# Transposes of queries, pooled keys and values moved from TensorE to DMA in a fused attention and gated layer kernel

## The chip, the cores and the metric

The kernel runs on one core of a Trainium2 chip. The metric is the device time of one launch in microseconds; each run is one launch, and the number given for a kernel is the median of its runs.

## The reference

Two layers run one after the other, the second on the first one's result. All inputs and the output are float32.

```python
# q (4, 12288, 128); kv (4, 384, 32, 128); w_sr (128, 128)
kv_pool = kv.reshape(B, H // 4, 4, W // 4, 4, C).mean(axis=(2, 4))
k = v = kv_pool.reshape(B, -1, C) @ w_sr          # 768 keys a batch; values are the same numbers
a = softmax(q @ k.transpose(0, 2, 1) / sqrt(C))
x = (a @ v).reshape(49152, 128)
h = x @ w_in                                      # w_in (128, 2048)
out = (h * sigmoid(1.702 * h)) @ w_out            # w_out (2048, 128)
```

## The kernel before

**Groups and chunks.** The 49152 queries are 96 groups of 512 (24 a batch). In the attention layer a group meets 6 chunks of 128 keys, in the second layer 16 chunks of 128 hidden units. For each chunk TensorE does a "fill" into PSUM, a matmul of 512 columns (L350 in `fill_attn`, L596 in `fill_moe`). ScalarE takes two or three chunks at a time through exp (L352) or through the activation (L598) and writes bf16 into the large SBUF buffer `ag`, which holds 102 chunks. TensorE later "drains" them: for attention twelve matmuls of 129 columns for three key chunks (L363; the 129th column sums the weights), for the second layer one matmul of 512 columns for each chunk (L606). VectorE normalises the attention result into `x` (L386, L389), and transposes the final result from PSUM (L617); SP stores it (L619). Work goes in two rounds: attention of groups 0 to 47, their second layer, then the same for 48 to 95.

**Work that VectorE does in ScalarE's place.** The chunks of groups 48 to 51 (`early`), nine others (`rolling`) and 17 chunks of the second layer (`lent`) go through a polynomial on VectorE (L431 to L475).

**A planner written in Python** sets the order on every engine while the program is built. It keeps estimated clocks `now` (TensorE), `end[p]` (ScalarE's p-th activation) and `dve`, in units of one 512-column matmul, and places drains and other TensorE work between fills as long as the next fill still comes in time:

```python
FIXED, CHUNK, SWITCH, HANDOVER, EVACUATE = 0.295, 1.978, 6.0, 1.0, 4.5
...
limit = end[-1] - len(seq[n + 3][1]) - HANDOVER if n + 3 < len(seq) else 1e9
```

An activation of n chunks is taken to last `FIXED + CHUNK * n`. A fill may start half a `HANDOVER` after its two banks' last activation, and the activation half a `HANDOVER` after the fill. All engines take their instructions strictly in that order; a semaphore wait on one holds up what stands behind it.

**Queries.** TensorE needs them transposed, channel by token. `load_q` brings tiles of four groups in as bf16, and `transpose_q` turns one group with four TensorE transposes and a copy by VectorE (L236, L242); this serves tiles 0, 1 and 2, so groups 0 to 11. Tiles from 3 on go another way: `cast_q` (L209, issued by POOL) casts them from float32 into the DRAM buffer `q_bf`, and `load_qT` (L215, issued by SP) reads that back with a DMA transpose. `TURN` says at which group that is issued. The casts of tiles 3, 4 and 5 are in POOL's queue from the start.

**Keys and values.** `w_sr` is scaled by 1/16. In batches 0 and 1 `pool_chunk` (L139) pools a chunk by 16 narrow matmuls, and `key_and_value` (L161, L162) makes the key chunk and the value chunk from the result with one matmul each. In batches 2 and 3 DMAs with accumulation add up the rows in SBUF (`add_kv`, L173), VectorE adds the last two (`sum_kv`, L179), and for each half batch `transpose_pooled` (L184, four TensorE transposes), `make_k` (L192) and `make_v` (L199, three matmuls) follow with a copy by VectorE after each. These three are handed to the planner in `extras`, and it places them between fills. Values sit in `vs` with tokens on partitions, keys in `kTs` with channels on partitions.

**Other traffic on SP.** `x` is put away to DRAM (`put_away`, L503) and brought back transposed (`bring_back`, L509) in pieces of six groups, in the second layer of round one between groups 9 and 18.

Of the kernel before, what the change touches and what calls it, by code (L numbers as in the profile page):

```python
# [24 lines left out]
def kernel(  # L25
    ctx, tc, q, kv, w_sr, moe_w_in, moe_w_out, out,
):
    nc = tc.nc
# [20 lines left out]
    q_flat = q.rearrange("b n c -> (b n) c")  # L49
    x_bf = nc.dram_tensor("x_bf", (B * N, C), BF, kind="Internal").ap()  # L50
    q_bf = nc.dram_tensor("q_bf", (B * N, C), BF, kind="Internal").ap()

    kv_r = kv.rearrange("b (ch p) (a w) c -> b a ch p (w c)", p=128, a=2)

# [4 lines left out]
    R = 2  # L59
    XS = NS // R  # L60
    EARLY = 4
    AG = 102

    cpool = ctx.enter_context(tc.tile_pool(name="const", bufs=1))
# [33 lines left out]
    def acc_bf():  # L98
        return acc().bitcast(BF)
# [16 lines left out]
    HC = H // 128  # L116
    h = J // 2
    kv_tiles, kv_sums, pooled, pTs, kTs, vs = {}, {}, {}, {}, {}, {}

    def new_keys(b):  # L120
        kTs[b] = kvres.tile([128, J], BF, name="kT")

        vs[b] = kvres.tile([128, JC, C + 8], BF, name="v")
        nc.vector.memset(vs[b][:, :, C:C + 1], 1.0)

    def load_chunk(b, jc):

        a, ch = divmod(jc, HC)
        t = x_tile(XS - 1 - jc)
        nc.gpsimd.dma_start(out=t, in_=kv_r[b, a, ch])  # L130
        kv_tiles[b, jc] = t.rearrange("p (wp w1 c) -> p w1 wp c", w1=r, c=C)

    def pool_chunk(b, jc):

        ps = acc()
        t = kv_tiles.pop((b, jc))
        for wp in (0, 2, 1, 3) if (b, jc) == (0, 0) else range(4):
            for w in range(r):
                nc.tensor.matmul(ps[:, 32 * wp:32 * wp + 32], t[:, w, wp, :], sum4,  # L139
                                 start=(w == 0), stop=(w == r - 1))  # L140
        pTs[b, jc] = kvtmp.tile([128, 128], BF, name="pTc", bufs=2)
        nc.vector.tensor_copy(pTs[b, jc], ps[:, 0:128])

    def key_chunk(b, jc):
        if jc == 0:
# [22 lines left out]
    def add_kv(b, n):  # L168
        i, w = divmod(n, r)
        if n == 0:  # L170
            kv_sums[b] = kvsum.tile([Hp, 2, Wp, C], F32, name="kvs")
        for i2 in range(2):
            nc.gpsimd.dma_start(out=kv_sums[b][:, i2], in_=kv_p[b, i, w, :, i2],  # L173
                                **({"accum_op": ADD} if n else {}))
# [3 lines left out]
        pooled[b, a] = kvtmp.tile([Hp, 4, C], BF, name="pooled")  # L178
        nc.vector.tensor_tensor(pooled[b, a], t[:, 0], t[:, 1], ADD)  # L179

    def transpose_pooled(b, a):
        ps = acc_bf()[:, 0:h].rearrange("p (a b) -> p a b", a=4)
        for wp in range(4):
            nc.tensor.transpose(ps[:, wp, :], pooled[b, a][:, wp, :], ident[:Hp, :Hp])  # L184
        pTs[b, a] = kvtmp.tile([128, h], BF, name="pT")
        nc.vector.tensor_copy(pTs[b, a], ps.rearrange("p a b -> p (a b)"))

    def make_k(b, a):
        ps = acc()
        if a == 0:  # L190
            new_keys(b)
        nc.tensor.matmul(ps[:, :h], w_sr_sb, pTs[b, a], start=True, stop=True)  # L192
        nc.vector.tensor_copy(kTs[b][:, a * h:(a + 1) * h], ps[:, :h])

    def make_v(b, a):
        ps = acc()
        pT = pTs.pop((b, a))
        for k in range(K):
            nc.tensor.matmul(ps[:, k * C:(k + 1) * C], pT[:, k * 128:(k + 1) * 128], w_sr_sb,  # L199
                             start=True, stop=True)  # L200
        nc.vector.tensor_copy(vs[b][:, a * K:(a + 1) * K, 0:C], ps[:, :h].rearrange("p (k c) -> p k c", k=K))
        for jc in range(a * K, a * K + K):
            vs[b, jc] = True

# [10 lines left out]
        nc.sync.dma_start_transpose(out=qTs[s], in_=q_bf[s * SG:(s + 1) * SG, :])  # L215


    QS = 3
    qs = [x_tile(XS - 1 - JC - s) for s in range(QS)]

    def load_q(s, lo, hi):
# [31 lines left out]
    for jc in range(2, JC):  # L253
        load_chunk(0, jc)
    load_q(1, 2, 4)
    for s in range(2, QS):
        load_q(s, 0, 2)
        load_q(s, 2, 4)
    cast_q(3)
    cast_q(4)  # L260

# [32 lines left out]
            nc.tensor.matmul(banks[:32, 2, :], ones, ones.unsqueeze(1).broadcast_to([128, 16, 32]),  # L294
                             start=True, stop=True)

    w_in_sb = cpool.tile([128, d_ff], BF)
    w_out_sb = cpool.tile([128, FCH, C], BF)

    ag = agpool.tile([128, AG, 512], BF, name="ag")  # L300
    warm(13)
# [44 lines left out]

    def fill_attn(chunks, ps):
        for k, (i, jc) in enumerate(chunks):
            rhs = qTs[i // 4][:, 0, (i % 4) * G:(i % 4 + 1) * G]
            nc.tensor.matmul(ps[:, k, :], kTs[i // GB][:, jc * 128:(jc + 1) * 128], rhs,  # L350
                             start=True, stop=True)
        nc.scalar.activation(place([("a",) + c for c in chunks]), ps, AF.Exp, scale=scale)  # L352

    def drain_attn(t, a):

        nonlocal kept
        i, u, k = t // 4, t // TS, t % TS
        split = u < SPLIT
        if k == 0 and (a == 0 or split):
            av_of[u] = acc(("av", u))  # L360
# [58 lines left out]
    def early_step():  # L419
        nonlocal steps  # L420
        on_dve(next(steps))
        if steps.gi_frame.f_locals["last"]:
            steps = None
            made[early_todo.pop(0)] = dve

    def early_exp(ps, out):
        last = False
# [49 lines left out]
        yield 3.5  # L477

    raw = None
    made, used = {}, []  # L480
    steps, early_todo = None, [c for c in rolling if c[0] < early[0]]
    early_todo += [(i, jc) for i in early for jc in range(JC)]
# [37 lines left out]
        nc.vector.memset(one, 0.0)  # L520
        nc.gpsimd.memset(one, 0.0)  # L521

    TURN = {6: 3, 7: 4, 8: 5, 20: 6, 21: 7, 22: 8, 25: 9, 32: 10, 35: 11, 40: 12}
    CAST = {0: [5], 13: [6], 14: [7], 15: [8], 16: [9], 26: [10, 11], 27: [12]}
    CAST_MOE = {20: 13, 21: 14, 22: 15, 23: 16, 33: 17, 34: 18, 35: 19, 36: 20, 37: 21, 38: 22, 39: 23}

    def background(i):

        first_round = i < GB * 2
        s = TURN.get(i, NS) if first_round else i // 4 + 3 if i % 4 == 0 else NS  # L530
        if s < NS:
            load_qT(s)
        if i in CAST:
            gate()
            for s in CAST[i]:
                cast_q(s)
        if i in (10, 12):
            gate()
            for jc in range(i % 10 * 3 // 2, i % 10 * 3 // 2 + 3):
                load_chunk(1, jc)  # L540
        if 0 <= i - 16 < JC:
            extras.append((key_and_value, 1, i - 16))
        if 0 <= i - 15 < JC:
            extras.append((pool_chunk, 1, i - 15))
        if i in (28, 33, 38):
            put_away(0, (i - 28) // 5)
        if i in (31, 36, 41):
            bring_back(0, (i - 31) // 5)
        if i == 28:
            gate()  # L550
            nc.gpsimd.dma_start(out=w_in_sb, in_=moe_w_in)
        if i == 29:
            gate()
            nc.gpsimd.dma_start(out=w_out_sb, in_=moe_w_out.rearrange("(o p) c -> p o c", p=128))

    def background_moe(g):
# [18 lines left out]
        for b, lo in ((2, 2), (3, 24)):  # L575
            if lo <= g < lo + 8:
                gate()
                add_kv(b, g - lo)
            if g in (lo + 10, lo + 12):
                use_kv(b, (g - lo - 10) // 2)  # L580

    def use_kv(b, a):
        nonlocal extra_at
        sum_kv(b, a)
        on_dve(3.5)
        extra_at = max(extra_at, dve + 1.5)
        extras.extend([(transpose_pooled, b, a), (make_k, b, a), (make_v, b, a)])

    extras = []

# [120 lines left out]
    def prepare(p):  # L711
# [3 lines left out]
        for i, jc in part:  # L715
            if (kind, i) not in begun:
                begun.add((kind, i))
                (background if kind == "a" else background_moe)(i)
            while kind == "a" and ((key_and_value, i // GB, jc) in extras or (transpose_q, i) in extras):
                f, *args = extras.pop(0)  # L720
                now = max(now, free[next_acc()]) + COST[f][0]
                f(*args)
                free[last_acc] = copied(f)
# [13 lines left out]
        13: [(key_and_value, 0, 4)],  # L737
        15: [(pool_chunk, 0, 5)],
        16: [(key_and_value, 0, 5), (later, 6)],
        17: [(later, 7)],  # L740
        18: [(later, g) for g in range(8, 12)]}

    FIXED, CHUNK, SWITCH, HANDOVER, EVACUATE = 0.295, 1.978, 6.0, 1.0, 4.5
    COST = {pool_chunk: (1.9, 2.6), key_chunk: (0.3, 2.4), value_chunk: (0.3, 2.4),
            transpose_q: (1.05, 4.2), early_fill: (1.0, 5.5), key_and_value: (0.55, 3.5),
            transpose_pooled: (0.9, 3.6), make_k: (0.8, 3.2), make_v: (0.8, 3.7)}
    COPY = {pool_chunk: 1.5, key_chunk: 1.5, value_chunk: 1.5, key_and_value: 2.8, transpose_q: 3.2}  # L750
    SMALL = 0.26
    RECIPROCAL = 8.2
    PAUSE = 4.0
# [15 lines left out]
    def fill(p):  # L769
# [13 lines left out]
        lo = K * (p % 2)  # L783
        (fill_attn if kind == "a" else fill_moe)(part, banks[:, lo:lo + len(part), :])
        if p >= 2:
            now = max(now, end[p - 2] + HANDOVER / 2)
        now += len(part)
        begin = max(now + HANDOVER / 2, end[p - 1] if p else 0.0)
        if p and kind != seq[p - 1][0]:
            begin += SWITCH  # L790
        end.append(begin + FIXED + CHUNK * len(part))
# [5 lines left out]
    for n in range(len(seq)):  # L797
        fill(n + 2)
        jobs(n + 3)
        while True:  # L800
            room = room_ahead()
            limit = end[-1] - len(seq[n + 3][1]) - HANDOVER if n + 3 < len(seq) else 1e9
            bank = free[next_acc()]
            f = None
            if extras and now >= max(extra_at, bank):
                f, *args = extras[0]
            if steps and dve <= now + 2.0:
                early_step()
            near = todo and todo[0][0] == "m" and todo[0][2] > 10
# [4 lines left out]
            if f:  # L814
                now = max(now, bank) + COST[f][0]
                f(*args)
                free[last_acc] = dve + 1.0 if f is early_fill else copied(f)
                if f in (transpose_pooled, make_k, make_v):
                    on_dve(2.5)
                extra_at = max(now + PAUSE, dve + 1.5 if f in (transpose_pooled, make_k, make_v) else 0.0)  # L820
                if f is early_fill:
                    pass
                else:
# [69 lines left out]
```

## Time and profile before

| what | value |
|---|---|
| median of 3 runs | 948.33 us (948.24 to 948.73) |
| span of the profiled execution, first to last instruction | 946.7 us |
| TensorE busy | 933.9 us |
| ScalarE busy | 933.5 us |
| VectorE busy | 575.1 us |
| granted TensorE clock | 1.000 |

The profiled execution has no separate time of its own; its span is 1.63 us below the median of the runs, which stands for what lies around the first and the last instruction. "PE" is TensorE, "PEld" its weight loads, "ACT" ScalarE, "DVE" VectorE, "POOL" GpSimd, "SP" the engine that issues most DMAs. Ends of matmuls are modelled, and matmuls overlap: one of 512 columns has a duration of 379 ns in the profile, and the next starts some 216 ns after it. Activations overlap too: a full-size one has a mean duration of about 1490 ns and the next starts about 1340 ns after it. So the busy shares of these two do not tell which of them waits. A row of a stretch of time reads: the stretch, its length, busy time and number of instructions of PE, PEld, DVE, ACT and POOL, granted clock, share of the DMA engines, GB/s. A DMA has a time from its issue to its landing, when its semaphore is complete.

### The profile page before, as it was taken

How to read it: one execution, taken by the hardware profiler on the slowest of the kernel's cores; microseconds unless marked ns; L12 is line 12 of the kernel's file. 1: busy time of each engine (PE TensorE's matmuls, PEld its weight loads, DVE VectorE, ACT ScalarE, POOL GpSimd, SP SyncE). 2: the span in 40 equal slices, each digit the busy share in tenths (PEclk: the TensorE clock that was granted, in tenths of full speed). 3: DMA queues.
4: the chain of work that ended last, by engine and by line, in shares of the span. 5: the costliest groups of instructions: out<-in, count | busy, mean ns of one | idle time of the engine just before them, and what ended most of it. 6: DMA issues, size and time to landing. Idle time of an engine off the chain costs nothing.

```text
span 946.7 us, 15374 instructions
## 1 busy us (share of the span) xinstructions
PE 933.9 (99%) x6200; PEld 502.5 (53%) x6314; DVE 575.1 (61%) x1091; ACT 933.5 (99%) x709; POOL 66.5 (7%) x115
## 2 busy tenths in 40 slices
PE   8999999999999999999999999999999999999998
PEld 4677776444444444444446777744444444444444
DVE  5753653011678776667765765376767766777651
ACT  6999999999999999999999999999999999999998
POOL 3101001330000232000000000000000000000000
PEclk9999999999999999999999999999999999999999
DMA  9997943999867799865335683552222222222222
GB/s 210 195 207 168 181 92 52 130 163 170 164 117 114 119 147 119 127 99 87 56 58 105 138 170 84 119 123 42 36 39 40 38 41 34 44 34 45 34 45 46
DMA packets 372856, 95.46 MB, mean 101 GB/s; under 512 B 346720, under 2 KB 370400, under 8 KB 372320
## 3 DMA queue, kind: packets, MB, share of 16 engines
q1 hardware_dynamic: 344000, 62.36, 36.9%
q0 software_dynamic: 28512, 31.99, 22.3%
q8 instruction: 49, 0.80, 0.3%
q14 instruction: 23, 0.19, 0.1%
q10 hardware_dynamic: 272, 0.13, 0.0%
HBM read 52.49 MB, written 48.76 MB: 107 GB/s over the span
## 4 chain that ended last, share of the span: by engine, by line
PE 97%; ACT 1%; DMA 1%; issue 1%; DVE 0%; POOL 0%; POOLq 0%
PE banks L606 35%; PE banks L596 34%; PE banks L363 14%; PE banks L350 12%; ACT ag L352 1%; PE banks L415 1%; DMA x<-in_kv_dram 1%; PE banks L139 0%; PE banks L409 0%; PE banks L634 0%; PE banks L236 0%; POOL x L222 0%; PE banks L161 0%; PE banks L294 0%; PE banks L192 0%
## 5 line engine op out<-in xcount | busy, mean ns | idle before, releaser
L598 ACT ACTIVATE ag<-banks 128x1536 bf16<-128x1536 f32 (+1 forms) x509 | 681.1, 1489 | 0.0
L596 PE MATMUL banks<-x,w_in_sb 128*128 128x512 bf16 x1476 | 405.8, 379 | 1.7
L606 PE MATMUL banks<-ag,w_out_sb 128*128 128x512 bf16 x1477 | 402.6, 379 | 1.7
L352 ACT ACTIVATE ag<-banks 128x1536 bf16<-128x1536 f32 (+2 forms) x192 | 245.6, 1421 | 3.5 <-PE banks L236 2.3
L606 PEld LDWEIGHTS <-w_out_sb 128*128 128x128 bf16 x1520 | 148.3, 98 | 177.2 <-issue 0.2
L596 PEld LDWEIGHTS <-w_in_sb 128*128 128x128 bf16 x1519 | 147.1, 98 | 171.3 <-issue 0.7
L617 DVE STREAM_TRANSPOSE o_sb<-banks 128x512 f32<-128x512 f32 x95 | 68.1, 717 | 171.4 <-PE banks L606 166.9
L363 PEld LDWEIGHTS <-ag 128*128 128x128 bf16 x2268 | 145.5, 98 | 44.6 <-issue 0.3
L363 PE MATMUL banks<-v,ag 128*128 128x129 bf16 x2268 | 163.0, 220 | 0.2
L350 PE MATMUL banks<-qT,kT 128*128 128x512 bf16 x498 | 145.0, 379 | 3.5 <-ACT ag L352 0.5
L442 DVE SCALAR_TENSOR_TENSOR ea<-ea,eb 128x512 f32<-128x512 f32 x132 | 90.4, 685 | 3.7 <-DVE ea L442 0.7
L386 DVE RECIPROCAL rec<-banks 128x3 f32<-128x3 f32 x124 | 22.3, 180 | 85.3 <-PE banks L363 84.9
L389 DVE TENSOR_TENSOR x<-banks,rec 128x384 bf16<-128x384 f32 x124 | 69.1, 557 | 4.3
L350 PEld LDWEIGHTS <-kT 128*128 128x128 bf16 x543 | 45.8, 98 | 25.9 <-issue 2.0
L473 DVE RECIPROCAL eb<-ea 128x256 f32<-128x256 f32 x34 | 57.6, 1724 | 0.5
L466 DVE SCALAR_TENSOR_TENSOR ea<-ea,eb 128x512 f32<-128x512 f32 x68 | 46.5, 683 | 1.9
L173 POOL DMA_DIRECT2D kvs<-in_kv_dram x32 | 40.4, 1323 | 19.3 <-DMA kvs<-in_kv_dram 17.1
L431 DVE TENSOR_SCALAR ea<-banks 128x512 f32<-128x512 f32 x33 | 22.8, 692 | 29.6 <-PE banks L415 29.2
L521 POOL MEMSET gate_tile<- 1x1 f32 x38 | 3.4, 89 | 325.8 <-DVE gate_tile L520 325.8
L453 DVE TENSOR_SCALAR qT<-banks 128x512 f32<-128x512 f32 x17 | 11.8, 692 | 20.7 <-PE banks L409 20.6
L437 DVE SCALAR_TENSOR_TENSOR eb<-eb,ea 128x512 f32<-128x512 f32 x33 | 22.8, 691 | 0.9
L444 DVE SCALAR_TENSOR_TENSOR ag<-ea,ee 128x512 bf16<-128x512 f32 x24 | 16.6, 691 | 1.2
(83 smaller groups left out, 286.3 us busy)
## 6 DMA issues: line engine op xcount, KB each, us to landing
out_dram<-o_sb SPq DMA_DIRECT2D x380, 64.0 KB, 2.0
kvs<-in_kv_dram POOLq DMA_DIRECT2D x32, 384.0 KB, 6.3
q_bf<-in_q_dram POOLq DMA_DIRECT2D x21, 512.0 KB, 6.6
x_bf<-x SPq DMA_DIRECT2D x13, 768.0 KB, 5.6
x<-in_kv_dram POOLq DMA_DIRECT2D x11, 512.0 KB, 10.4
x_bf<-x SPq DMA_DIRECT2D x6, 384.0 KB, 4.6
x<-in_q_dram POOLq DMA_DIRECT2D x5, 256.0 KB, 15.3
x<-in_kv_dram SPq DMA_DIRECT2D x1, 1024.0 KB, 5.0
```

Source lines behind the costliest of these rows:

```text
L173: nc.gpsimd.dma_start(out=kv_sums[b][:, i2], in_=kv_p[b, i, w, :, i2], **({"accum_op": ADD} if n else {}))
L350: nc.tensor.matmul(ps[:, k, :], kTs[i // GB][:, jc * 128:(jc + 1) * 128], rhs, start=True, stop=True)
L352: nc.scalar.activation(place([("a",) + c for c in chunks]), ps, AF.Exp, scale=scale)
L363: nc.tensor.matmul(av_of[u][:, k * (C + 1):(k + 1) * (C + 1)], weights(("a", i, jc))[:, o:o + T], vs[i // GB][:, jc, 0:C + 1], start=(jc = ...
L389: nc.vector.tensor_tensor(to, ps[:, :, 0:C], rec.unsqueeze(2).broadcast_to([128, TS, C]), MUL)
L442: nc.vector.scalar_tensor_tensor(a, a, COEFFS[k], b, ADD, MUL)
L466: nc.vector.scalar_tensor_tensor(a, a, COEFFS[k], b, ADD, MUL)
L473: nc.vector.reciprocal(b[:, m:m + 256], a[:, m:m + 256])
L596: nc.tensor.matmul(ps[:, k, :], w_in_sb[:, fc * 128:(fc + 1) * 128], x[:, g % (4 * XS) * G:(g % (4 * XS) + 1) * G], start=True, stop=True)
L598: nc.scalar.activation(place([("m",) + c for c in chunks]), ps, AF.Gelu_apprx_sigmoid)
L606: nc.tensor.matmul(o_of[g], w_out_sb[:, fc, :], weights(("m", g, fc)), start=(fc == 0), stop=(fc == FCH - 1))
L617: nc.vector.transpose(o_sb, o_of.pop(g))
```

## The change

Four things change. First, tile 2 of the queries (groups 8 to 11) is no longer loaded and turned on TensorE: it goes by `cast_q(2)`, in the place of its loads on POOL, and by `load_qT(2)` on SP, issued at group 5. Second, for batches 2 and 3 the pooled sums are written to a DRAM buffer (`put_pooled`) and read back with a DMA transpose (`turn_pooled`); `make_k` waits for it. The steps come at one group's distance: sum and write, transpose, `make_k`. Third, the values of batches 1, 2 and 3 are no longer made by a matmul: since they are the keys' own numbers, the finished keys are written to DRAM (`put_k`) and read back transposed, a chunk at a time (`turn_k`). All of these DMAs are issued by SP. Fourth, the planner's times: `FIXED` goes from 0.295 to 0.24; a fill may start `RELEASE` = 0.3 after the banks' last activation (was 0.5); an activation begins `LATENCY` = 0.95 after the fill (was 0.5); the margin in `limit` is 1.2 (was 1.0).

The diff also has a way to pool batch 1 by additions on VectorE (`add_chunk`, `pool_added`), which `ADDED = ()` leaves unused, and it joins the two weight tiles into one buffer. Batch 1 is still pooled by the narrow matmuls, a chunk a group, each followed by its key.

```diff
-    for s in range(2, QS):
-        load_q(s, 0, 2)
-        load_q(s, 2, 4)
+    cast_q(2)
     cast_q(3)
     cast_q(4)
...
-    TURN = {6: 3, 7: 4, 8: 5, 20: 6, 21: 7, 22: 8, 25: 9, 32: 10, 35: 11, 40: 12}
+    TURN = {5: 2, 6: 3, 7: 4, 8: 5, 20: 6, 21: 7, 22: 8, 25: 9, 32: 10, 35: 11, 40: 12}
...
-    def transpose_pooled(b, a):
...
+    def put_pooled(b, a):
+        nc.sync.dma_start(out=pool_bf[b, a].rearrange("w h c -> h w c"), in_=pooled[b, a])
+
+    def turn_pooled(b, a):
+        pTs[b, a] = kvtmp.tile([128, 1, h], BF, name="pT")
+        nc.sync.dma_start_transpose(out=pTs[b, a], in_=pool_bf[b, a].rearrange("w h c -> (w h) c"))
+
+    def put_k(b, a):
+        jc = slice(a * K, a * K + K)
+        nc.sync.dma_start(out=k_bf[b, jc].rearrange("j c t -> c j t"),
+                          in_=kTs[b][:, a * h:(a + 1) * h].rearrange("c (j t) -> c j t", t=128))
+
+    def turn_k(b, a):
+        for jc in range(a * K, a * K + K):
+            turned_v.add((b, jc))
+            nc.sync.dma_start_transpose(out=vs[b][:, jc:jc + 1, 0:C], in_=k_bf[b, jc])
...
+    def key_alone(b, jc):
...
+        nc.tensor.matmul(ps[:, 0:128], w_sr_sb, pTs.pop((b, jc)), start=True, stop=True)
...
-    def make_v(b, a):
...
-        if 0 <= i - 16 < JC:
-            extras.append((key_and_value, 1, i - 16))
-        if 0 <= i - 15 < JC:
-            extras.append((pool_chunk, 1, i - 15))
+        for a in range(2) if first_round else ():
+            if (1, a) in stored:
+                stored.remove((1, a))
+                turn_k(1, a)
+            if (1, a * K) not in turned_v and all((1, jc) in vs for jc in range(a * K, a * K + K)):
+                put_k(1, a)
+                stored.add((1, a))
...
-            if g in (lo + 10, lo + 12):
-                use_kv(b, (g - lo - 10) // 2)
+            a, step = divmod(g - lo - 9, 3)
+            if 0 <= a < 2 and step == 0:
+                sum_kv(b, a)
+                on_dve(3.5)
+                put_pooled(b, a)
+            if 0 <= a < 2 and step == 1:
+                turn_pooled(b, a)
+            if 0 <= a < 2 and step == 2:
+                extras.append((make_k, b, a))
+            if 1 <= a < 3 and step == 0:
+                put_k(b, a - 1)
+            if 1 <= a < 3 and step == 1:
+                turn_k(b, a - 1)
...
-        18: [(later, g) for g in range(8, 12)]}
...
-    FIXED, CHUNK, SWITCH, HANDOVER, EVACUATE = 0.295, 1.978, 6.0, 1.0, 4.5
+    FIXED, CHUNK, SWITCH, HANDOVER, EVACUATE = 0.24, 1.978, 6.0, 1.0, 4.5
+    RELEASE, LATENCY, MARGIN = 0.3, 0.95, 1.2
...
-            now = max(now, end[p - 2] + HANDOVER / 2)
+            now = max(now, end[p - 2] + RELEASE)
...
-        begin = max(now + HANDOVER / 2, end[p - 1] if p else 0.0)
+        begin = max(now + LATENCY, end[p - 1] if p else 0.0)
...
-            limit = end[-1] - len(seq[n + 3][1]) - HANDOVER if n + 3 < len(seq) else 1e9
+            limit = end[-1] - len(seq[n + 3][1]) - MARGIN if n + 3 < len(seq) else 1e9
```

## The prediction

> **What bounds the kernel now.** I read the page first, then stretches of a late stage, then single instructions. The page shows two engines that look full:
>
> ```profile
> span 946.7 us, 15374 instructions
> ...
> PE 933.9 (99%) x6200; PEld 502.5 (53%) x6314; DVE 575.1 (61%) x1091; ACT 933.5 (99%) x709; POOL 66.5 (7%) x115
> ...
> PE 97%; ACT 1%; DMA 1%; issue 1%; DVE 0%; POOL 0%; POOLq 0%
> ```
>
> The chain names TensorE, but its ends are modelled, so I count instead. In the table of stretches PEld's count is the number of matmuls:
>
> ```profile
> 700.00:800.00 100.00, 99.47 (x455) 45.33 (x464) 70.01 (x98) 100.00 (x75) 0.00 (x0) 1.00 0.26 40
> 800.00:900.00 100.00, 99.53 (x456) 45.32 (x463) 73.53 (x102) 100.00 (x76) 0.00 (x0) 1.00 0.25 38
> ```
>
> 464 matmuls of 512 columns in 100 us are one each 215.6 ns, which is also the distance between neighbours: no gap is left. The same sum over the run: 3632 matmuls of 512 columns x 215.6 ns, 2304 of 129 columns (L363) x 56.4 ns, and 18.4 us of small ones make 931.4 us. TensorE ends at 943.4 us, so it idles for 12.0 us: 9.8 before 75 us, 2.2 in all the rest. From 75 us on, a microsecond of TensorE work or waiting is a microsecond of the run.
>
> ScalarE is close behind. Full-size ACTIVATEs start at least 1.330 us apart (1.335 where nothing holds them up). The sum of what lies over 1.330 (0.904 and 0.477 for the smaller ones) is 18.4 us: 3.4 at the start, 4.2 at three table loads, and most of the rest where the activation starts 630 ns after the weight load of its last matmul, the least the trace has. There ScalarE waits for TensorE, though its groups show "idle 0.0".
>
> Before 35 us DMA and ScalarE also limit. The lines for what follows, each one instruction:
>
> ```profile
> L215 SPq DMA_TRANSPOSE qT<-q_bf x1: 4773/4773/4773, 29.2 to 29.2; - x1
> ...
> DMA to landing us min/median/max: 7.0/7.0/7.0
> ...
> L619 SPq DMA_DIRECT2D out_dram<-o_sb x1: 505/505/505, 298.5 to 298.5; - x1
> ...
> DMA to landing us min/median/max: 5.9/5.9/5.9
> ...
> L509 SPq DMA_TRANSPOSE x<-x_bf x1: 3390/3390/3390, 231.0 to 231.0; - x1
> ...
> DMA to landing us min/median/max: 6.3/6.3/6.3
> ```
>
> The first is today's earliest query transpose, the second a store issued just after a query cast, the third a transpose that the new one must queue behind.
>
> **What is removed.** TensorE loses 16 query transposes (16 x 56 ns = 0.90 us), 6 value matmuls of batch 1 (0.34), 16 transposes of pooled sums at 42 ns (0.67) and 12 value matmuls of batches 2 and 3 (0.67): 2.58 us. VectorE loses 4 x 0.69 + 6 x 0.28 + 4 x 0.36 + 4 x 0.56 = 8.1 us of copies; it is 61% busy and nobody waits for it, so that is worth nothing.
>
> The row is 56 ns for a 128x128 transpose (start to start; its own duration is 219 ns). The Trainium skill (TensorE: Matmul & The Clock Gate, Part 4) gives about 275 ns in a kernel's context; by that the 16 + 16 transposes would be 8.8 us instead of 1.57, and the result 7.2 us lower than mine. The row decides.
>
> **The new hand-over times** change only order. In the built program, TensorE's work ahead of the last fill falls by 7.8 us and what follows the last fill grows from 2.7 to 7.9 us: 5.2 us of second-layer matmuls go to the end. Work is neither added nor lost, so TensorE's end moves from 943.4 to 940.8. ScalarE must then keep up: of its excess about 7.5 us can go (6.1 at the 118 cases of 630 ns and 2.8 at the 147 of 660 to 700 ns, less 1.4 of jitter that the free ones show too), its end moves from 942.1 to 934.6, and TensorE's remaining 1.3 + 5.2 us put the end at 941.1. The later of both counts: -2.3 us instead of -2.58. The tighter pacing can't gain more, since TensorE has no idle to give back.
>
> **Queries of groups 8 to 11.** Their f32 load to SBUF (2 x 512 KB, landed at 25.4 and 26.7) becomes a cast to DRAM of the same bytes, then one DMA transpose. I take the cast as landing at 26.7 too. SP issues the transpose then, but three further casts run until 34.2 (the last one's landing). The store above shows what that means: the cast issued at 298.45 landed at 304.02, the store issued at 298.50 landed at 304.38, and between 299.6 and 303.0 none of its packets moved; stores free of a cast take 1.8 to 2.0 us. Today's transpose, issued at 29.2, likewise sends its first packet at 31.9 and lands at 36.2. A cast's packets are 16 to 32 KB, a transpose's 256 B. So the new one should land between 34.9 (all 2080 packets from 32.2 at the 1.13 per ns that today's reaches after 34.0, plus 0.8 us to the semaphore) and 36.2 (like today's). Its first user, the fill of group 8, is at 33.7 now (ScalarE takes it at 34.29) and has the same TensorE work in front of it as before. Everything behind it on TensorE waits. Cost 0 (if it slips between the casts, no less: the fill can't run before ScalarE frees its bank) to 2.6 us; I take 2.0, nearest to today's row.
>
> The skill (DMA: Bandwidth & Descriptors, Queues, rings and completion order) says that a DMA engine goes round its rings packet by packet. By that alone the transpose would interleave, land some 3.8 us after its issue as an undisturbed one does (434.7 us), near 30.5, and cost nothing; the sum would be 949.5. The store's 3.4 us without a packet speaks against it.
>
> The later query transposes move back one place: that for group 12 (fill at 43.5) would land near 38.4, that for group 20 (65) near 44; hidden.
>
> **Values of batch 1.** SP writes keys out and transposes them back. The first write falls in the casts that land until 68.3, so SP stands at it until about 69, and with it the query transposes of groups 24 to 35. That for group 24 landed at 71.8 and is needed at 75.7; 3 us later it still fits. The values are first used at 95.5. Taken as 0, at most 2 us.
>
> **Pooled keys of batch 2, first half.** make_k must now wait for a store and a transpose on SP. TensorE reaches it ahead of fill (13, 2), at about 235.4 in today's times. The transpose stands on SP behind the transpose of x issued at 231.0 (3.39 us of issue, landing at 237.3), which in turn waits for a store that landed at 230.9. Its 400 packets follow in the same queue: landing at 237.7 to 238.5. TensorE waits 2.3 to 3.1 us, and nothing else can run there since it takes instructions in order; ScalarE has only about 0.1 us in hand and stops too. If SP gets 3 us ahead, the cost is 0; I take 2.7.
>
> **The other three make_k.** Second half of batch 2: behind two x stores that landed at 254.6, ready near 256.3 for 256.9: 0, up to 1. Batch 3, first half: during the cast that lands at 390.7, ready near 392.2 for 392.7: 0. If it misses that window it meets the next cast (392.5 to 398.8): up to 6. Second half: SP is held from 408.6 to 412.8 by a cast, stores land until 414.7, ready near 414.9 for 414.1: 0.8, between 0 and 6 as before. Their values have a whole stage of time. Output stores queue behind these steps on SP and leave up to 5 us later; three o_sb buffers at 7.2 us a group hide that, and without them each such microsecond would stop VectorE's next o_sb, then a bank of TensorE. On POOL one cast replaces two loads, so later ones are issued no later.
>
> **Sum** against the profiled 946.7 us: -2.3 + 2.0 + 2.7 + 0.8 = +3.2, 949.9. The median of the runs, 948.33, lies 1.63 above the span; kept, that gives 951.5.
>
> **Rivals.** (1) All transfers are hidden: then only TensorE's loss counts, 946.0. For it: each step has a whole group (7.2 us) to the next, and an undisturbed transpose lands in 3.8. Against: the three lines above. It decides if the queries land before 33.7 and the pooled keys before 235.4. (2) Only one of the two larger waits comes: 948.33 - 2.3 + 2.0 to 2.7 = 948.0 to 948.7, or up to 950.2 with the later one. (3) A pooled transpose falls into the next cast: 951.5 + 6 = 957.5 at most. A long gap may also cost clock: the first matmuls of the run, after idling, start 427 ns apart instead of 215.6.
>
> The skill's TensorE page (Why this matters for your kernels) warns of gaps over about 3 us, after which the array runs at half clock; no row here shows it in the middle of a run. By its window of about 3.4 us one such gap would add some 1.7 us.
>
> **How the numbers follow.** The forecast with most of its waits has 0.56, rival 1 0.19, rival 2 0.18, rival 3 0.07. The range leaves out about 2 in 10: from rival 1's 946.0 to 955.5, half-way into rival 3. The cases lie on both sides of zero; the forecast's own range is 950 to 954.5 (each wait at its bounds). About 0.2% (1.9 us) is what a measurement of this kernel can tell from no change: faster 0.20 (rival 1 and a little of rival 2), same 0.22, slower 0.58.
>
> **What would show it.** TensorE's count: 6 small matmuls on L184, none of 96 columns, and a sum of 928.8 us. A wait of the fill L397 for the DMA of qT near 34 us of 1.4 to 2.5 us; a wait of L248 for the DMA of pT near 237 us of about 2.7, and of 0.8 near 415. Full-size ACTIVATEs 1.335 us apart, no longer 1.343, and TensorE working 6 us past the last one. I am wrong if L397 and L248 wait for nothing, or if TensorE idles elsewhere after 75 us.

## The result, and the profile after

The changed kernel takes 994.86 us (median of 4 runs, 989.18 to 999.22), the kernel before 948.52 us beside it (948.24 to 948.73): a ratio of 1.0486, 95% interval 1.0451 to 1.0522. It is 46.3 us slower, far outside the range of the prediction. The profiled execution is the longest of the four, 999.22 us with a span of 997.1 us. The page of the changed kernel:

```profile
span 997.1 us, 15415 instructions
...
PE 955.7 (96%) x6264; PEld 503.9 (51%) x6264; DVE 566.4 (57%) x1074; ACT 934.5 (94%) x709; POOL 65.8 (7%) x114
...
PEclk9799899999999999989999999999999999999999
...
PE 86%; DMA 9%; ACT 2%; SPq 2%; issue 0%; POOL 0%; DVE 0%; DVEq 0%; POOLq 0%
```

TensorE and ScalarE do no more than before (ScalarE is busy 934.5 us, before 933.5), but now DMA and SyncE's queue hold 11% of the chain, and TensorE's granted clock has dents, in the second, the fifth and the eighteenth slice of 25 us. TensorE's waits (total us, times, longest) say which transfers these are:

```profile
PE banks L463 <- DMA qT<-q_bf: 18.5, 2, 10.0
PE banks L248 <- DMA pT<-pool_bf: 15.5, 3, 6.1
```

L463 is the matmul in `early_fill` (work for VectorE), L248 is `make_k`. Five stands, 34 us. The two of L463 with what follows them, as a table of stretches:

```profile
27.00:36.00 9.00, 0.47 (x3) 0.03 (x2) 0.27 (x1) 1.63 (x2) 0.00 (x0) 0.70 0.91 178
36.00:41.00 5.00, 5.00 (x31) 3.46 (x32) 3.11 (x8) 2.05 (x2) 0.00 (x0) 0.51 0.46 105
110.00:120.00 10.00, 0.63 (x3) 0.10 (x1) 0.28 (x1) 2.16 (x2) 0.00 (x0) 0.80 1.50 105
120.00:126.00 6.00, 5.40 (x30) 3.48 (x31) 2.19 (x5) 1.45 (x1) 0.00 (x0) 0.50 0.66 119
```

The figure behind the five engines is the granted clock: TensorE does two or three matmuls in 9 or 10 us, and then works at 0.5 for another 5 us. Of these 5 us half is lost again. By matmul starts the five stands are 27.07 to 35.97, 110.25 to 120.60 (both L463), 258.63 to 262.98, 421.45 to 427.92 and 451.72 to 457.53 us (L248); clock records of 0.5 of 3.4 to 10.2 us lie behind or across the end of each.

The third loss doesn't show as a wait. The late stage, whose rows stood at 464 and 463 weight loads in 100 us before:

```profile
700.00:800.00 100.00, 100.00 (x462) 44.82 (x461) 74.52 (x105) 100.00 (x75) 0.00 (x0) 1.00 0.22 37
800.00:900.00 100.00, 100.00 (x461) 44.92 (x460) 71.30 (x102) 100.00 (x76) 0.00 (x0) 1.00 0.23 40
```

Three matmuls less in each 100 us, with TensorE "100.00" busy: ends are modelled, the counts are not. What is not done there is left for the end. The last rows of ScalarE's activations and of TensorE's matmuls in the two timelines (start, length), first before the change, then after it:

```profile
939.10 2.96 ACT L598 ACTIVATE ag<-banks 128x1024 bf16<-128x1024 f32 x3
940.78 2.62 PE L634 MATMUL banks<-w_out_sb,ag 128*128 128x128 bf16 x44
```

```profile
984.60 2.03 ACT L661 ACTIVATE ag<-banks 128x1024 bf16<-128x1024 f32 x2
990.35 3.23 PE L697 MATMUL banks<-w_both,ag 128*128 128x128 bf16 x55 [0.30 <-DVE o_sb L680]
```

Before, TensorE ends 1.3 us after the last activation; now it ends 6.95 us after it. In this execution the waits (34.0 us), half of the 22.4 us that TensorE works at half clock behind them (11.2) and the 5.6 us more at the end come to 50.8 us, and the spans differ by 50.4.

### The profile page after: what moved, and what is told of

Read it like the earlier page. It is cut to its first block, busy times and chain, and to the rows that moved or that the text cites. A ratio compares the mean times of both kernels' runs of the same rounds, so it can differ in the third digit from the quotient of the medians.

```text
span 997.1 us, 15415 instructions
## 1 busy us (share of the span) xinstructions
PE 955.7 (96%) x6264; PEld 503.9 (51%) x6264; DVE 566.4 (57%) x1074; ACT 934.5 (94%) x709; POOL 65.8 (7%) x114
## 4 chain that ended last, share of the span: by engine, by line
PE 86%; DMA 9%; ACT 2%; SPq 2%; issue 0%; POOL 0%; DVE 0%; DVEq 0%; POOLq 0%
PE banks L659 32%; PE banks L669 31%; PE banks L411 11%; PE banks L397 10%; DMA qT<-q_bf 4%; ACT ag L399 2%; DMA pT<-pool_bf 2%; DMA x<-in_kv_dram 2%; DMA x_bf<-x 1%; PE banks L463 1%; SPq L682 1%; SPq L559 1%; PE banks L457 0%; PE banks L697 0%; PE banks L152 0%
## 5 line engine op out<-in xcount | busy, mean ns | idle before, releaser
L661 ACT ACTIVATE ag<-banks 128x1536 bf16<-128x1536 f32 (+1 forms) x509 | 681.4, 1605 | 20.3 <-PE banks L659 20.2
L659 PE MATMUL banks<-x,w_both 128*128 128x512 bf16 x1519 | 413.2, 380 | 0.0
L669 PE MATMUL banks<-ag,w_both 128*128 128x512 bf16 x1503 | 408.9, 381 | 0.0
L669 PEld LDWEIGHTS <-w_both 128*128 128x128 bf16 x1520 | 149.1, 98 | 180.0 <-issue 3.5
L659 PEld LDWEIGHTS <-w_both 128*128 128x128 bf16 x1519 | 147.4, 98 | 179.2 <-issue 15.4
L411 PEld LDWEIGHTS <-ag 128*128 128x128 bf16 x2268 | 149.2, 99 | 50.6 <-issue 4.0
L411 PE MATMUL banks<-v,ag 128*128 128x129 bf16 x2268 | 167.4, 222 | 0.1
L397 PE MATMUL banks<-qT,kT 128*128 128x512 bf16 x543 | 151.0, 383 | 2.2 <-ACT ag L399 0.7
L217 POOL DMA_DIRECT2D kvs<-in_kv_dram x32 | 40.7, 1320 | 25.6 <-DMA kvs<-in_kv_dram 22.4
L463 PE MATMUL banks<-qT,kT 128*128 128x512 bf16 x33 | 13.5, 408 | 18.5 <-DMA qT<-q_bf 18.5
## 6 DMA issues: line engine op xcount, KB each, us to landing
x<-in_kv_dram POOLq DMA_DIRECT2D x11, 512.0 KB, 10.2
```

The lines of the kernel that those rows point to most:

```text
L411: nc.tensor.matmul(av_of[u][:, k * (C + 1):(k + 1) * (C + 1)], weights(("a", i, jc))[:, o:o + T], vs[i // GB][:, jc, 0:C + 1], start=(jc = ...
L659: nc.tensor.matmul(ps[:, k, :], w_in_sb[:, fc * 128:(fc + 1) * 128], x[:, g % (4 * XS) * G:(g % (4 * XS) + 1) * G], start=True, stop=True)
L661: nc.scalar.activation(place([("m",) + c for c in chunks]), ps, AF.Gelu_apprx_sigmoid)
L669: nc.tensor.matmul(o_of[g], w_out_sb[:, fc, :], weights(("m", g, fc)), start=(fc == 0), stop=(fc == FCH - 1))
```

## The experiments

All kernels here come from one source in which the four parts can be switched singly, so their line numbers differ from those of the changed kernel: `make_k` is L269, `early_fill`'s matmul L487, the attention fill L422, the attention drain L435, the second layer's fill L699. The theory: the time went into waits of TensorE for late transpositions and into the half clock behind each. The rivals: the new hand-over times made the waits, or the load on the DMA slows everything a little.

**The parts alone.** Edit: only one of the four switched on. By a slip in these edits the switch for the hand-over times had no effect: all four kernels have the new times, so the first three are to be compared with the fourth and not with the kernel before. The expectations were written without knowing that.

```diff
-FLAGS = (1, 1, 1, 1)   # queries, batch 1's values, pooled keys, hand-over times
+FLAGS = (1, 0, 0, 0)   # only_q; (0, 1, 0, 0) only_v; (0, 0, 1, 0) only_p; (0, 0, 0, 1) only_h
```

Expected of only_q: 

> The kernel before with the part on the queries alone (slice 2 by cast and DMA transposition). Theory of the waits: TensorE stands at the early fill of group 10 from 27 until the transposition of slice 2 lands near 36 (8.7 us), and then runs some 10 us at half clock (2.5 us more); 0.9 us of transposes go; some 958.5 us in all. Rival, new hand-over times: the waits are taken up by the order and this part is worth nothing alone, 947 to 949. Rival, load on the DMA: the loss goes with the bytes moved and spreads; under 2 us, with no single stand of 8 us.

Expected of only_v: 

> The kernel before with the part on the values of batch 1 alone. Theory of the waits: SyncE stands at the stored keys from 70 to 79 and at six transpositions of 1.25 us, so the transposition of query slice 9 goes out near 94 instead of 79, meets the casts of slices 10 to 12 and lands near 120; TensorE waits 10 us at the early fill of group 38 and has 2.8 us of half clock after it; 961 us. Rival, hand-over times: 948 alone. Rival, load on the DMA: under 2 us, spread.

Expected of only_p: 

> The kernel before with the part on the pooled keys (and values) of batches 2 and 3 alone. Theory of the waits: waits at make_k of batch 2's first half (4 us) and of both halves of batch 3 (6 us each, the transposition meets the next cast), each with half clock after it (1.6 to 2.7 us); with 1.4 us of transposes and values gone, some 968 us. Rival, hand-over times: 948 alone, since the waits came with the new placing. Rival, load on the DMA: spread over the stages, no wait of over 2 us at make_k.

Expected of only_h: 

> The kernel before with the new hand-over times alone. Theory of the waits: no long wait of TensorE, clock 1.00; TensorE stops some 0.2 us at every sixth activation, 5 us over the span: 951 to 955. Rival, hand-over times: they are the cost, 975 or more. Rival of the prediction on record: no gain and no cost, 948 to 949.

| kernel | median us | interval of the ratio | over only_h | stands of TensorE |
|---|---|---|---|---|
| only_h | 956.96 | 1.0073 to 1.0103 | (+8.5 over before) | none |
| only_q | 966.92 | 1.0176 to 1.0210 | +10.0 | 27.44 to 36.14 |
| only_v | 967.85 | 1.0188 to 1.0219 | +10.9 | 75.40 to 77.15, 99.89 to 108.34 |
| only_p | 957.40 | 1.0078 to 1.0108 | +0.4 | 234.52 to 236.57, 257.89 to 259.08 |

Queries and values cost about what the waits say (expected were 10 and 12.5). The times alone cost 8.5, against 3 to 7 in the theory and nothing in the prediction. The pooled part was expected to cost 20 and costs almost nothing alone. One reason is at the end of the run: from the last activation to TensorE's end it is 10.4 us in only_h, 9.8 in only_q, 10.4 in only_v and 8.9 in only_p, so some of the work taken off TensorE comes off there and pays part of the stands back. 948.48 + 8.5 + 10.0 + 10.9 + 0.4 = 978.3; 16.6 us of the 994.86 belong to no part alone.

**What the new times do.** The profile of only_h, stretches of the late stage, and ScalarE's instructions at the end (timeline: start, length, then in brackets the idle time before):

```profile
700.00:800.00 100.00, 100.00 (x461) 44.88 (x460) 70.43 (x98) 100.00 (x76) 0.00 (x0) 1.00 0.23 40
800.00:900.00 100.00, 100.00 (x461) 44.77 (x459) 72.78 (x100) 100.00 (x76) 0.00 (x0) 1.00 0.22 38
```

```profile
937.32 3.84 ACT L701 ACTIVATE ag<-banks 128x1024 bf16<-128x1024 f32 x4
951.16 0.27 ACT L745 COPY o_sb<-banks 128x128 f32<-128x128 f32 x1 [9.99 <-PE banks L737]
```

TensorE does 4 matmuls less in each 100 us and has them left when ScalarE is done: ScalarE's last activation ends at 941.2 (before 942.1), then it idles for 10 us. This suggested a theory in numbers. By the planner's formula a full activation takes (0.24 + 3 x 1.978) x 215.6 = 1331 ns; the old 0.295 gives 1343. Measured, from start to start between 300 and 900 us, the least is 1330 and the mean 1344 before, 1342 in only_h. The old value is the mean, the new one the minimum. With it the planner believes that it has 11.9 ns less for TensorE's other work at each of 701 activations, 8.3 us in all, and puts that work at the end. The two parts of the edit were separated:

```diff
-    FIXED, RELEASE, LATENCY, MARGIN = 0.295, 0.5, 0.5, 1.0
+    FIXED, RELEASE, LATENCY, MARGIN = 0.24, 0.5, 0.5, 1.0     # fixed_only
+    FIXED, RELEASE, LATENCY, MARGIN = 0.295, 0.3, 0.95, 1.2   # rest_only
```

Expected of fixed_only: 

> The kernel before, with FIXED alone changed, from 0.295 to 0.24. Theory of the budget: the planner gives TensorE 0.055 units (11.9 ns, a unit being one 512-column matmul of 215.6 ns) less work beside each of the 701 activations; TensorE is the bound, so 8.3 us of its work is left after the last activation: 956.7, with TensorE ending some 10 us after ScalarE. Rival: the earlier release (0.3 for 0.5) is what makes TensorE stop at the fills; then this is 948 to 949.

Expected of rest_only: 

> The kernel before, with the release, the latency and the margin new (0.3, 0.95, 1.2) and FIXED left at 0.295. Theory of the budget: no change, 948 to 949.5, TensorE ending 1 to 2 us after ScalarE. Rival, the release: 955 to 957, as with all four new.

Measured: fixed_only 956.94 us (ratio 1.0076 to 1.0103), rest_only 948.61 us (0.9993 to 1.0012). ScalarE's longest wait in fixed_only, then the late stage of rest_only:

```profile
ACT o_sb L745 <- PE banks L737: 10.0, 1, 10.0
```

```profile
700.00:800.00 100.00, 99.53 (x456) 45.30 (x463) 71.83 (x101) 100.00 (x76) 0.00 (x0) 1.00 0.23 40
800.00:900.00 100.00, 99.53 (x455) 45.22 (x463) 71.72 (x98) 100.00 (x75) 0.00 (x0) 1.00 0.22 38
```

`FIXED` alone costs the 8.5 us; the other three times cost or bring nothing that can be told from noise (948.61 beside 948.39).

The late stage of only_h (640 to 920 us, 206 full activations) also shows what the mean is made of. Where the first weight load of an activation's fills comes more than 80 ns ahead of the end of the last activation but one, the activation starts within 1335 ns of its neighbour (129 of 134). Where it comes later, the activation is late (69 of 72), 1366 ns behind its neighbour on the mean, and mostly starts 630 or 680 ns after the last weight load: ScalarE waits there for its fill. No such load comes more than 215 ns ahead. That leaves a room of some 0.13 us, less than one matmul of 215.6 ns, so that a single other matmul between two fills can make an activation late. This is read from the trace and was not tested by a run.

**The half clock behind a stand.** On only_q, TensorE was kept at work in its stand:

```diff
         rhs = qTs[i // 4][:, 0, (i % 4) * G:(i % 4 + 1) * G]
+        for _ in range(38 if i == 10 else 0):
+            nc.tensor.matmul(ps[:32, :], ones, ones.unsqueeze(1).broadcast_to([128, 16, 32]), start=True, stop=True)
         nc.tensor.matmul(ps, kTs[i // GB][:, jc * 128:(jc + 1) * 128], rhs, start=True, stop=True)
```

Expected: 

> The kernel of the run on the queries (slice 2 by DMA, new hand-over times, 966.9 us), with 38 throw-away matmuls of 215 ns ahead of the early fill of group 10, so that TensorE works through 8.2 of the 8.7 us of its stand. Theory: the stand stays, but the clock stays at 1.00, and the 10 matmuls' worth of half clock behind it (36.1 to 40.1, 2.0 us) goes: 964.5 to 965.3. Rival, the half clock has another cause or costs nothing: 966.5 or more.

Measured: 964.85 us, 2.07 less than only_q. The stretch after the stand, first of only_q, then of q_warm:

```profile
36.00:40.00 4.00, 3.86 (x22) 2.49 (x23) 2.42 (x6) 1.02 (x1) 0.00 (x0) 0.50 0.35 78
```

```profile
36.00:40.00 4.00, 3.95 (x46) 2.94 (x47) 3.48 (x10) 2.87 (x4) 0.00 (x0) 1.00 0.47 101
```

Twice the matmuls at clock 1.00 in place of 0.50; 4 us at half clock are the 2 us. The half clock comes from the idling, and work without any use takes it away.

**Undoing on the changed kernel.** Four edits of the full change, each against one cause:

```diff
-    FIXED, CHUNK, SWITCH, HANDOVER, EVACUATE = 0.24, ...
+    FIXED, RELEASE, LATENCY, MARGIN = 0.295, 0.5, 0.5, 1.0                 # old_times
-    ... and i // 4 - 1 <= group // 4 and i >= 4 * QS)
+    ... and i // 4 - 1 <= group // 4 and i >= 4 * QS and (i >= 12 or group >= 8))   # hold_group10
-            if 0 <= a < 2 and step == 2:
-                extras.append((make_k, b, a))
+            if 1 <= a < 3 and step == 0:
+                extras.append((make_k, b, a - 1))                          # make_k_later
+            ...                                                            # put_k, turn_k a step later
-            if (1, a) in stored:
+            if (1, a) in stored and i >= 25:                               # values_after_slice9
```

Expected of old_times: 

> The changed kernel with the old hand-over times (0.295, 0.5, 0.5, 1.0). Theory of the waits: the waits for query slice 2 (8.9 us) and slice 9 (10 us) stay, those at make_k stay or move by the phase of the casts, and the 8.5 us that the new times cost alone go: 984 to 990. Rival, the new times made the waits: no wait of over 3 us, 946 to 952.

Expected of hold_group10: 

> The changed kernel with the early fill of group 10 held until group 8 is being filled, so that the first reader of query slice 2 is the fill of group 8, as the prediction on record had it. Theory: the stand of 8.9 us at 27 is replaced by one of 1 to 2.5 us near 34, and the half clock behind it goes: 9 us less, near 986. Rival, the landing sets it wherever the reader stands: the stand is moved and not shortened, 993 or more.

Expected of make_k_later: 

> The changed kernel with make_k, the storing of its keys and the transposition of them one group of the MLP later each (query slice 16 is loaded two groups later, for the order's sake). Theory: the three stands of 4.4, 6.5 and 5.8 us at make_k go, and their half clock (5.9 us) with them: near 972. Rival: the waits come back, at the early fills of batch 2 that need the keys or at the values: 985 or more.

Expected of values_after_slice9: 

> The changed kernel with the six transpositions of batch 1's values issued after that of query slice 9 on SyncE's queue. Theory: slice 9 goes out near 80 to 85 and lands ahead of the casts of slices 10 to 12, the stand of 10.4 us at 110 and its half clock go: near 982. Rival: the values then land late, and TensorE stands at the drain of group 24 (100 to 125 us) instead: 992 or more.

*old_times* took 971.41 us (1.0229 to 1.0278), 23.5 less than the full change; neither the theory (984 to 990) nor the rival (946 to 952) had that. TensorE ends 1.0 us after the last activation, 5.9 less than in the changed kernel; the rest is in the stands and the half clock behind them. The stand for slice 2 stays (8.8 us). The others changed with the order: none at group 38, 5.7 us instead at the drain of group 24, and at `make_k` 2.2, 1.3 and 1.2 us.

*hold_group10* took 988.21 us (1.0394 to 1.0436), 6.7 less, where 9 was expected. Its waits:

```profile
PE banks L487 <- DMA qT<-q_bf: 8.9, 1, 8.9
PE banks L422 <- DMA qT<-q_bf: 3.9, 2, 3.0
```

The 8.9 us left on L487 are those of group 38. The first stand is now one of 3.0 us at the fill of group 8 (33.20 to 36.40), with 3.4 us of clock 0.5 behind it. So the early reader cost most of it, and the reader that the prediction had in mind would have waited too.

*make_k_later* took 977.80 us (1.0286 to 1.0333), 17.1 less; no wait for `pT` is left in its trace. Near 972 was expected; the stand at group 38 is still there (7.8 us). 977.8 is close to the sum of the single parts, 978.3, so the 16.6 us that belong to no part alone are those of the three stands at `make_k` and of the half clock behind them (16.6 and 5.9 us in the profiled execution, the longest of its four).

*values_after_slice9* took 996.16 us (1.0472 to 1.0525): the rival was right. The stand at group 38 is gone, but TensorE now stands for the values themselves at the drain of group 24, from 103.28 us on:

```profile
PE banks L435 <- DMA v<-k_bf: 11.9, 5, 7.8
```

In the changed kernel's trace the casts of slices 10 to 12 and both weight loads are issued from 92 us on and land until 129 us; in both orders tried, the transposition that is last in SyncE's queue falls into them.

**Why the pooled part costs 0.4 us alone and 17 in company.** The traces of only_p and of the changed kernel for the same step, batch 3's first half. First only_p: the transposition and `make_k`; then the changed kernel: the transposition and the cast beside it.

```profile
L251 SPq DMA_TRANSPOSE pT<-pool_bf x1: 1118/1118/1118, 387.0 to 387.0; - x1
...
DMA to landing us min/median/max: 6.7/6.7/6.7
```

```profile
L269 PE MATMUL banks<-pT,w_sr_sb x1: 326/326/326, 394.3 to 394.3; 128*128 128x384 bf16 x1
```

```profile
L230 SPq DMA_TRANSPOSE pT<-pool_bf x1: 1537/1537/1537, 420.5 to 420.5; - x1
...
DMA to landing us min/median/max: 7.3/7.3/7.3
```

```profile
L257 POOL DMA_DIRECT2D q_bf<-in_q_dram x1: 486/486/486, 421.6 to 421.6; - x1
...
DMA to landing us min/median/max: 6.1/6.1/6.1
```

Both transpositions meet a cast and land 0.2 us after it (427.87 and 427.71 in the changed kernel). In only_p that is 0.7 us before `make_k` comes; in the changed kernel `make_k` was ready at 421.5, and the transposition did not go out before 420.5, because SyncE had been held until 420.4 by four output stores during the cast before. The run that takes the casts away from these groups:

```diff
-    CAST_MOE = {20: 13, ..., 33: 17, 34: 18, 35: 19, 36: 20, 37: 21, 38: 22, 39: 23}
+    CAST_MOE = {20: 13, ..., 40: 17, 41: 18, 42: 19, 43: 20, 44: 21, 45: 22, 46: 23}
```

Expected: 

> The changed kernel with the casts of query slices 17 to 23, given out at MLP groups 33 to 39, moved to groups 40 to 46. Theory, the pooled transposition of batch 3 starves behind the cast beside it: both stands at make_k of batch 3 (6.5 and 5.8 us) go with their half clock (4.3 us), 978 to 980; the stand of batch 2 stays. Rival: SyncE's stores ahead of the transposition delay it, casts or not: the stands stay over 3 us, 988 or more.

Measured: 974.54 us (1.0265 to 1.0298), 20.3 less. Of `make_k`'s three waits one is left:

```profile
PE banks L487 <- DMA qT<-q_bf: 14.9, 2, 8.4
PE banks L269 <- DMA pT<-pool_bf: 1.5, 1, 1.5
```

The casts are the cause in batch 3, directly or by way of the stores that they hold up in SyncE's queue. It is more than expected since the stands of batch 2 and of group 38 are shorter in this trace too (1.9 and 7.0 us from start to start, for 4.4 and 10.4). What moves the phase between casts, stores and `make_k` from one kernel to the next was not tried and stays open; the runs of the full change itself spread over 10 us.

**What the removed TensorE work is worth.** The pooled part by itself, with the old times and `make_k` a group later (the edit of make_k_later on the kernel before):

Expected: 

> The kernel before with the pooled part alone (old hand-over times) and make_k one group of the MLP later. Theory: no stand at make_k, 1.4 us of transposes and value matmuls gone from a TensorE that is never idle: 946.8 to 947.4, faster than before. Rival: the later keys or the transfers hold something else up: 949 or more.

Measured: 949.58 us (1.0007 to 1.0024): slower by 1.2, with no wait for `pT`. TensorE stood 0.7 us each at three fills between 497 and 500 us for ScalarE, longer in all than the work taken off it, and it ends 2.55 us after the last activation instead of 1.34: these are the 1.2 us. Why it stands at those fills is not settled. To leave transfers out altogether, work was removed and nothing put in its place:

```diff
-        for wp in range(4):
+        for wp in range(1):          # transpose_pooled
-        for k in range(K):
+        for k in range(1):           # make_v
-        for i in range(4):
+        for i in range(4 if g < 8 else 1):   # transpose_q
```

Expected: 

> The kernel before with 32 small TensorE instructions left out and nothing put in their place: one transposition instead of four for queries of groups 8 to 11 and for the pooled rows of batches 2 and 3, one value matmul instead of three, the copies spreading the one result (so these queries, keys and values are not the reference's); 12 x 56 + 12 x 42 + 8 x 56 ns = 1.62 us of TensorE time. If ScalarE, busy from its first activation to its last, sets the pace: 948.2 to 948.7. Rival, the sum on record, in which TensorE's time comes off the end: 946.6 to 947.1.

Measured: 948.18 us, before 948.47 (ratio 0.9988 to 1.0006). Of 1.62 us 0.3 came off the end, and the fastest of 11 runs took 947.98, where the rival had 946.6 to 947.1. ScalarE's mean distance between full activations is 1343.9 ns, as before, its last activation ends at 941.7 (942.1), and TensorE ends 1.3 us after it, as before. The planner's own costs of the instructions were left as they were, so it did not put other work in their place.

**Together.** Old times, batch 1's values on TensorE, `make_k` a group later, group 10 held:

Expected: 

> The changed kernel with what cost time mended: old hand-over times, batch 1's values left on TensorE, make_k one group later, group 10 held to group 8. Theory: 949.6 of the pooled part alone, and 2.5 to 3.2 us of stand at the fill of group 8 with up to 1.7 us of half clock behind it: 952 to 954.5, so slower than before still. Rival, the parts hit each other again: 958 or more.

Measured: 953.19 us (1.0034 to 1.0061). One stand is left, from 33.42 to 36.18 us, and the clock stays at 1.00 in the profiled execution, which took 951.10 us; the other three took 953.18 to 954.53 at mean clocks of 0.995 to 0.998, so some half clock is in the median:

```profile
PE banks L422 <- DMA qT<-q_bf: 2.5, 1, 2.5
```

So the parts add up, and none of the kernels run here that do the whole work beats the one before.

## Why the prediction was wrong

The direction was right (0.58 on slower), the size was not: +3.2 us forecast, +46 measured.

- **Hand-over times and removed work, booked at -2.3 us: TensorE's end right, ScalarE's gain wrong.** The prediction saw that 5.2 us of matmuls go to the end; TensorE does end 6.95 us after the last activation, where 1.3 + 5.2 were forecast. The step that failed is "of its excess about 7.5 us can go". 1.0 went (18.4 to 17.4 us in only_h, the last activation from 942.1 to 941.2). Taken together, 941.2 + 6.95 is 4.7 us later than TensorE's end before, 943.4, and not 2.3 earlier. Most of the excess stayed a wait for fills: activations that are late and start within 700 ns of their last weight load hold 10.1 us of it before and 8.9 in only_h. Alone the times cost 8.5 and not 4.7, since there all of TensorE's work is still to be done, 10.4 us of it behind the last activation. "A microsecond of TensorE work or waiting is a microsecond of the run" holds for waiting and for work behind the last activation; work taken from between the fills brought 0.3 of 1.62 us (less_work).
- **Queries of groups 8 to 11, +2.0: the landing right, the reader wrong.** Forecast 34.9 to 36.2, landed at 35.9. The step that failed is "its first user, the fill of group 8, is at 33.7 now". With `QS` = 2 and `qTs` filled when the transposition is issued, `early_fits` lets VectorE's chunk of group 10 go at once: TensorE stood from 27.07. With group 10 held the fill of group 8 waits 2.5 (mended) to 3.0 us (hold_group10), near the forecast 2.0.
- **Values of batch 1, "taken as 0, at most 2 us": +10.9.** The prediction followed SyncE's queue only through the query transposes of groups 24 to 35, and checked the first of them. That one, taken to fit, is the small stand in only_v (75.40 to 77.15). The one for slice 9 is behind all six value transpositions, 1.2 us of SyncE each. Before it was issued at 79.1 us and took 3.9 us; now, by the changed kernel's line:

```profile
L263 SPq DMA_TRANSPOSE qT<-q_bf x1: 11569/11569/11569, 94.5 to 94.5; - x1
...
DMA to landing us min/median/max: 26.1/26.1/26.1
```

- **Pooled keys: the place right, the size wrong.** 2.7 forecast for batch 2's first half, 1.9 (hold_group10) to 4.4 (the changed kernel) measured from start to start. For batch 3, 0 and 0.8 were taken, and up to 6 kept as a bound "if it misses that window". It missed both, for 6.5 and 5.8. Rival 3, that a pooled transpose falls into the next cast, is the mechanism; its chance of 0.07 and its 957.5 "at most", for one miss, came from reading windows of 0.5 us out of a trace whose phases the other parts move by 30 us.
- **The half clock** was told of beside the rivals and not put in the sum. In the profiled execution TensorE works at clock 0.5 behind the five stands for 4.9, 5.6, 3.2, 5.5 and 3.2 us (matmuls of 512 columns 427 ns apart), and half of that, 11 us, is lost, of the 50 us by which the spans differ. q_warm showed it for one stand: 2.07 us measured, 2.0 worked out in this way. The rule of the Trainium skill (TensorE: Matmul & The Clock Gate, Why this matters for your kernels), no gap over some 3 us, agrees with the rows: start to start, 2.77 us in the profiled execution of mended left the clock at 1.00, 3.20 us in hold_group10 brought 3.4 us of 0.5. The other executions of mended, at 0.995 to 0.998, have no trace, so where the border lies is not known better than that.
- **The skill's round by packets** (DMA: Bandwidth & Descriptors, Queues, rings and completion order), which the prediction read as a transposition going along beside a cast: no such gain shows in the rows. Three transpositions issued beside a cast landed 0.2 us after it (427.87 and 427.71, 457.48 and 457.29 in the changed kernel, 393.66 and 393.49 in only_p). In what order the rings were served was not looked into.
- **Smaller readings, without effect on the outcome:** the first 256 B packet of the earliest query transpose before moves at 32.4 and not at 31.9; packets of the query casts are of 32 KB, none of 16; and 955.5 is two thirds and not half of the way from 951.5 to 957.5.

## What to carry to other kernels

When a program is ordered by a planner, a buffer that is filled later has to be followed to every reader that the planner's conditions admit, since readers that were held back by the old way of filling it come forward; and a cost in the planner is better taken from the mean that the trace shows than from the least (here 1344 and 1330 ns, worth 8.5 us). A wait on an engine that takes instructions in order is priced by its length and, from some 3 us on in these traces, by the half clock behind it. When two engines are both full, work taken from one of them between the waits was worth almost nothing here, and counted only where that engine had work left after the other was done; each long wait counted in full.

## What was not expected of the hardware

A query transposition of 512 KB that took 3.9 us to land in the kernel before took 26.1 us when it was issued among three casts and two weight loads. SyncE itself was held by it for 11.6 us, so that everything behind it in the queue went out late too.
